# A new written-out order for an RWKV attention with Fourier mixing, and a last output tile in two halves

## The chip, the cores and the metric

The kernel runs on one core of one Trainium2 chip. The time is that of the device for one execution, in microseconds (us), as the median of several runs. A profile is taken of one execution by the hardware profiler, and its time is given beside its span, the time from the first to the last instruction. The engines are TensorE (PE, matmuls), VectorE (DVE), ScalarE (ACT), GpSimd (POOL) and SyncE (SP, which here only issues DMAs).

## The reference

Inputs are r, k and v of 4 batches, 8 heads, 768 tokens and 48 channels, a decay w and a bonus u per head and channel, and the weights of an MLP. The first part is a linear attention with a decaying state, the second a Fourier mixing over tokens and channels, a normalisation and an MLP with a residual:

```python
for t in range(S):
    cur = np.einsum('bhd,bhe->bhde', u[None] * kt, vt)
    y[:, :, t] = np.einsum('bhd,bhde->bhe', rt, state + cur)
    state = w[None, :, :, None] * state + np.einsum('bhd,bhe->bhde', kt, vt)
...
x = np.ascontiguousarray(attn_out.transpose(0, 2, 1, 3)).reshape(B, S, H * D)
X = np.fft.fft(np.fft.fft(x, axis=1), axis=2)
u = x + np.real(X).astype(np.float32)
un = (u - mu) / np.sqrt(var + 1e-06)
ch = np.maximum(un @ w_ch1, 0.0) @ w_ch2
return (u + ch).astype(np.float32)
```

The output has 4 x 768 rows of 384 columns in f32; the hidden layer of the MLP has 1536 columns.

## The kernel before

**Attention.** Each batch is cut into 6 chunks of 128 tokens, so there are chunks 0 to 23, six for each batch. For a chunk SP loads k, r and v (192 KB each; a ring of four buffers for k with r, and one of four for v). In the first twelve chunks DVE multiplies k and r by powers of the decay in two steps, KK (line 337) and KR (line 341); from chunk 12 on in one step, KR (line 330). Up to chunk 14 PE turns both round (tp, line 357) into one PSUM buffer, and two copies bring them to SBUF: KT, the keys (line 372), and KRT, the row copy of r, which also changes the order of the tokens by a strided access (line 375). From chunk 15 on SP's DMA transposes do this. V is a cast of v to bf16 (line 349 on ACT, 350 on DVE). PE forms the scores A (line 392) in two PSUM buffers; each half is masked into MA, on DVE straight from PSUM (line 404), or on POOL (line 401) after a copy AC by ACT (line 399). PR (line 382) is a product that gives the bonus term; de (lines 456 and 461), y (line 481), TT (lines 469 and 472), DE and xt put the chunk's result together in PSUM, and X (line 490 on DVE, 493 on ACT) brings it out in bf16. The state S is updated by u (line 424) and copied by DVE (line 438) or ACT (line 436).

**Mixing.** DVE folds X over tokens and channels by sums and differences: HH (line 510) and XF (line 524) for batch 0; EO (line 544), HH (line 550) and XF (lines 558 and 563) for the others. The matmuls fp (line 601) with the table te transform over tokens, TT2 copies the result out (line 610 on ACT, 613 on DVE), TR is that result reversed (line 620 on DVE, 624 on ACT), and mp (line 641) with the table hid transforms over channels. A batch gives two halves of three tiles. UF (lines 654 and 660) adds the residual X; where ACT does it, a matmul xr (line 652) adds X in PSUM first. UB is the normalised bf16 copy, and st and MV the statistics, either bn_stats and bn_aggr on DVE or a square with a sum on ACT (line 674). UNT is UB turned round, by PE (tq, line 685) in batch 0 and by SP's DMA transposes in the others.

**MLP.** Each of the 8 halves (numbers 0 to 7, two for a batch) has 12 times hp (three matmuls with W1, line 733) and HT, the ReLU (line 738 on ACT, 741 on DVE), and three output tiles: mo (12 matmuls with W2, line 753), osb on DVE (line 760) and the output DMA from SP (line 764). The two weight matrices come in by three POOL DMAs each (line 791), and each of these waits for the data of a certain chunk by a small copy before it (line 790). Most PSUM tiles of the mixing and the MLP share a ring of three buffers named mm.

**The order.** Nothing is scheduled while the kernel is built. Every operation is recorded with `op(...)`: a name, an engine, a planned duration, and other forms on other engines. It is then emitted in the order of a text:

```python
def _order(sch):
    return [(int(t.split(".")[0]), int(t.split(".")[1]) if "." in t else 0) for t in ORDER.split()]
...
        for n, a in order:
            o = self.ops[n]
            ...
            o["alts"][a][3]()
```

A token such as 226.1 stands for operation 226 in its other form, so the text sets both the order on every engine's queue and which engine does the work. Each engine takes its instructions in the order of emission. Operations 0 to 89 are filler matmuls on zeros (`idle`, line 211); those whose number is in the text are run.

Of the kernel before, what the change touches and what calls it, by code (L numbers as in the profile page):

```python
# [15 lines left out]
B = 4  # L16
# [3 lines left out]
DM = 384  # L20
# [73 lines left out]
106 93 144 90 94 113 101 120 95 110 118 146 97 137 102 91 92 115 98 0 105 103 114 104 1 143 96 140 116 147 117 2 107 99 108 112 111 3 149 109 4 5 150  # L94
119 6 121 7 130 152 124 8 122 128 9 125 148 10 221 129 11 222 100 145 126 132 224 123 241 151 133 242 12 13 225 14 153 226.1 15 131 142 227 228 155
139 134 127 244 265 231.1 235 223 232.1 16 156 236.1 17 245 233 246.1 18 229 158 234 19 20 135 237.1 248 230 136 154 138 141 239.1 251.1 266 238 21
157 243.1 268 249 247 253 252.1 22 159 269 250 23 270.1 24 254.1 25 289 272 161 240.1 290 26 273.1 275 255 274.1 162 292 267 256.1 276 257.1 27 160
293 277 271 259.1 291 258 278 28 163 260.1 309 301 294 310 279 164 302.1 296 333 312 280 218 297.1 298.1 299 281 29 30 313 314.1 31 165 334 283 282
311 316 315 321 167 295 317.1 336 335 261 32 284 300 337 33 34 338.1 319 303 285 35 168 262 322.1 304.1 36 305.1 37 981 38 219 318.1 307.1 306 220 263
340 170 264 39 355 341.1 166 308.1 725 286 726 343 342.1 320 323 739 718 324.1 325.1 344 732 740 719 327.1 339 326 356 733 328.1 288 287 345 329 171  # L100
734 330 720 346.1 741 347.1 727 169 332 349.1 331 348 375 721 350.1 173 742 722 395 743 735 736 174 352 728 351 729 357 353 354 376 172 723 744 737
724.1 980 367 745 730 176 738.1 731 358 396 368.1 177 748 746 754 377 747 749 755.1 179 750 760 982 756.1 387 761 762 774 388.1 775.1 359.1 780 776.1
751.1 786 781 757.1 360 787 763.1 768 415 777 378 782 180 769.1 983 362 379 788 175 794 365 783.1 772 789 770 795 361 796 773.1 771 366 369 363 797
798 370 986 799 380 364 752.1 1010 381 178 398 416 764.1 753.1 181 1008 399.1 371 987 765.1 382 1009 1040 397.1 400 373 383.1 384.1 407 385 372 418
435 1011 402 436 419 1002 1041.1 405.1 403 386 1026 408 420 182 404 1012 374 1027 438 1003 406.1 183 389 439 417.1 422 401 184 390 1000 421 437 425.1
423.1 426.1 1013 391 427 185 988 465 440.1 1006 428.1 441 186 424.1 393.1 984 392 989 447 1001.1 394.1 442 188 448.1 463 1034 464 443 189 409 1035.1
466 410 758.1 411 1007.1 1038 445 467.1 759.1 998 413 487 1039 412 766.1 1022 999 414 468 996 488.1 1023 429 469 497 997 191 470 767 444 498 430 778.1
1036 471.1 431 473.1 474.1 192 992 784.1 779.1 489 505 790.1 187 785.1 433.1 994 490 791.1 1037.1 446 432 190 995.1 1014 985 434.1 472.1 993 507 194
792.1 449 1015 491 492 508.1 195 450 1004 451 495.1 493 496.1 1028 197 1005 509 1024 1029 523 453.1 452 1025 1016 454.1 793 494 990 1017 475 455 991
1078 541 476 506 515 198 456 510 524 1079 477 511.1 512.1 513 543 516.1 457 525 458 479.1 478 526 193 1018 459 196 461 460 480.1 1019 558 199 583 533  # L110
499 528 500 1066 200 482 529 481 1080 531 501 201 1067 542 1020 484 560 545 462 559 1068 532 503.1 502 800 801 504.1 483 808 202 804 584 485 805 517
1081 486 809 534 530 802 518 806 810 803 550 514 807.1 811 203 812 604 813 546 814 1042 815 204 816 548 544 818 206 551 519 817.1 1043 819 820 1069
527 567 821 824 1044 549 521.1 568.1 585 520 825 826 547 830 522.1 839 831 561 605 851 840 832 207 562 827 852 552 1021 841 565.1 833 845 613 853
843.1 1030 846 847 838 553 842 844.1 1031 854.1 822.1 848.1 586 859 828.1 823.1 566.1 1054 554 834.1 829.1 556 555 563 205 1032 1055 835.1 849.1 1045
557 836.1 621 587 850.1 855.1 535 1046 590 1056 856.1 209 1074 536 614 1047 537 1076 857.1 208 1075.1 588 1070 858 539 1077.1 210 1082 1071 837 638
1098 1083 606 1106 1099 1084 1107 538 212 1085.1 1060 622 564 213 540 1048 589 1061 1062 1049 639.1 569 591 1063 630 640 1096 631.1 655 1110 1097 1108
607 1033 1111 1058 570 1109 211 571 1094 1059 1112 1095 573 672 1100 623 1113 572 608 1101 574 1052 611.1 609 612.1 214 1086 1053 217 575 592 1087
1072 576 656 1050 641 1073 1057 577 642 593 1051 578 1064 645.1 643 674 646.1 594 647 1088 1065 648 1114 596 1089 579 215 582 216 580 595 581 1102 673
597 610 599 1115 598 601 600 1103 603 602 1116 644 615 1126 657 616 1104 697 1127 1117 675 1105 860 861 617 1128 862 864 865 863 866 625 624 619 1129
867 618 628.1 872 698.1 626 873 620 874 868 869 875 876 870 1150 629.1 627 871 877 878 658 1151 879 880 881.1 882.1 649 1152 884 699 650 659 883.1 651  # L120
885 886 890 662.1 660 899 891 892 1153 653 664 887 661 900 905 901 893 911 906 907 652 902 912 1138 898 913 903.1 908.1 1090 914 904.1 665 909.1 663.1
919 1139 894.1 654 910.1 915.1 700 895.1 676 1140 683 916.1 917.1 679.1 677.1 1091 678.1 1141 684 888.1 685 680.1 1118 889.1 896.1 1092 687 686 1134
1119 918 688 1093 1122 1135.1 632 1123.1 1154 633 897 634 701 1155.1 1120 702.1 704 636 681 635 1121 1142 705 637 682.1 1130 703.1 1143 666 1146
1131.1 667 668 1148 1147 1178 1149 670 669 1132 1179 671 1124 1133 689 706 1125 690 1144 707 1136 691 1145 1170 692 1137 1162 708 1171.1 693 1168 710
696 709 695 1163 1169 694 711 1174 713 712 1164 1175 714 1165 715 717 920 716 921 928 1176 922 929 930 923 932 1177 933 931.1 934 924 925 935 926 1158
927 1172 1159 936 938 937 1173 944 939 940 945.1 950 946.1 1182 951 952 941 1160 947.1 1183 953.1 959 1161 965 958 960 961 942.1 971 966 967 1186 962
972 943.1 973 968 1187 954.1 974.1 979 963.1 955.1 1156 1188 975.1 964.1 1180 1157.1 1189 948.1 1184 976.1 1181.1 1166 1185 949.1 1190 969.1 1167.1
1204 1191.1 956.1 970.1 977.1 1208 1205.1 1196 957 1209 978 1216 1197 1226 1217 1214 1227 1220 1215.1 1228 1221 1194 1229.1 1206 1195 1202 1207 1192
1203 1232 1193 1198 1233.1 1199 1218 1200 1234 1219 1201 1235 1256 1236 1210 1257 1237 1211 1240 1212 1246 1241.1 1213 1247 1252 1248 1250 1253.1 1249
1238 1251 1230 1239 1258 1231 1259 1242 1260 1244 1243 1261 1270 1245 1254 1266 1255.1 1271 1267 1272 1273 1262 1268 1269 1222 1223 1263 1224 1225  # L130
1264 1265
"""


# [5 lines left out]
def kernel(  # L140
# [177 lines left out]
    def attend(i):  # L318
# [45 lines left out]
        else:  # L364
# [5 lines left out]
            else:  # L370
                def keys(copy):
                    return lambda: copy(KRT()[:, 0], tp()[:, 0])
# [467 lines left out]
```

## Time and profile before

| What | Value |
|---|---|
| Median of 5 runs | 181.57 us (180.8 to 183.18) |
| Profiled execution | 180.8 us, span 178.8 us, mean granted TensorE clock 0.996 |
| PE busy | 163.9 us (92%), of this 13.1 us filler matmuls (40 instructions) |
| DVE busy | 140.7 us (79%) |
| ACT busy | 118.8 us (66%) |
| POOL busy | 43.9 us (25%) |
| DMA | 26.84 MB moved, mean 150 GB/s |

Busy times are sums over the whole span; the share of an engine in one stage can be quite different, so the prediction reads them by stage. Times within the run are counted from the start of the span. Matmul records are pipelined, and one lasts longer than the time from its start to the next start.

### The profile page before, as it was taken

How to read it: one execution, taken by the hardware profiler on the slowest of the kernel's cores; microseconds unless marked ns; L12 is line 12 of the kernel's file. 1: busy time of each engine (PE TensorE's matmuls, PEld its weight loads, DVE VectorE, ACT ScalarE, POOL GpSimd, SP SyncE). 2: the span in 40 equal slices, each digit the busy share in tenths (PEclk: the TensorE clock that was granted, in tenths of full speed). 3: DMA queues.
4: the chain of work that ended last, by engine and by line, in shares of the span. 5: the costliest groups of instructions: out<-in, count | busy, mean ns of one | idle time of the engine just before them, and what ended most of it. 6: DMA issues, size and time to landing. Idle time of an engine off the chain costs nothing.

```text
span 178.8 us, 4317 instructions
## 1 busy us (share of the span) xinstructions
PE 163.9 (92%) x1628; PEld 108.4 (61%) x1628; DVE 140.7 (79%) x338; ACT 118.8 (66%) x290; POOL 43.9 (25%) x66
## 2 busy tenths in 40 slices
PE   5877968898999999999999899999999999999991
PEld 2344646675766666677666567766667765656560
DVE  5699899998999999999975999998696972232222
ACT  2897973399999994689989634595834997313200
POOL 6011335025344640742151133304210000000000
PEclk9999999999999999999999999999999999999998
DMA  3999899999999998999999998283002170022122
GB/s 81 240 219 223 193 277 213 212 229 226 198 183 178 181 185 160 181 207 244 150 241 215 141 208 215 45 189 101 0 0 91 29 149 0 18 73 88 44 88 88
DMA packets 88900, 26.84 MB, mean 150 GB/s; under 512 B 80432, under 2 KB 88240, under 8 KB 88880
## 3 DMA queue, kind: packets, MB, share of 16 engines
q1 hardware_dynamic: 86176, 23.77, 61.9%
q0 software_dynamic: 2144, 2.36, 8.2%
q10 hardware_dynamic: 560, 0.44, 0.8%
q8 instruction: 12, 0.20, 0.5%
q14 instruction: 8, 0.07, 0.1%
HBM read 20.08 MB, written 4.72 MB: 139 GB/s over the span
## 4 chain that ended last, share of the span: by engine, by line
PE 56%; DVE 15%; DMA 11%; ACT 8%; issue 3%; SPq 2%; POOL 2%; ACTq 0%; DVEq 0%; POOLq 0%
PE mm L753 23%; PE mm L733 19%; DMA W<-in_moe_w_ch_dram 4%; DMA vt<-in_v_dram 4%; PE mm L641 4%; PE mm L601 3%; DMA lw<-in_w_dram 3%; DVE MA L404 2%; SPq L306 2%; PE A_ps L392 2%; DVE KRT L375 2%; DVE PR L382 2%; DVE HH L550 1%; PE yd_ps L481 1%; DVE KR L341 1%
## 5 line engine op out<-in xcount | busy, mean ns | idle before, releaser
L733 PE MATMUL mm<-UNT,W 128*128 128x384 bf16 x288 | 53.4, 326 | 0.8 <-ACT DE L467 0.6
L753 PE MATMUL mm<-W,HT 128*128 128x384 bf16 x288 | 51.0, 326 | 0.4 <-DMA W<-in_moe_w_ch_dram 0.4
L738 ACT ACTIVATE HT<-mm 128x384 bf16<-128x384 f32 x71 | 34.1, 495 | 15.8 <-PE mm L733 15.7
L753 PEld LDWEIGHTS <-HT 128*128 128x128 bf16 x288 | 27.3, 98 | 17.4 <-issue 0.7
L733 PEld LDWEIGHTS <-W 128*128 128x128 bf16 x288 | 26.6, 97 | 17.1 <-issue 1.1
L469 POOL TENSOR_TENSOR TT<-V,DE 128x384 bf16<-128x384 bf16 x19 | 16.8, 884 | 48.9 <-ACT DE L467 48.2
L760 DVE SCALAR_TENSOR_TENSOR osb<-mm,rstd,UF 128x384 f32<-128x384 f32 x24 | 14.6, 614 | 14.9 <-PE mm L753 14.9
L401 POOL TENSOR_SCALAR_AFFINE_SELECT MA<-AC 128x512 bf16<-128x512 bf16 x26 | 18.7, 729 | 28.6 <-ACT AC L399 22.2
L741 DVE TENSOR_SCALAR HT<-mm 128x384 bf16<-128x384 f32 x25 | 13.3, 551 | 7.3 <-PE mm L733 7.2
L399 ACT CAST AC<-A_ps 128x512 bf16<-128x512 f32 x26 | 15.3, 593 | 2.6 <-PE A_ps L392 2.3
L674 ACT ACTIVATE lw<-UF,sm 128x384 f32<-128x384 f32 x24 | 14.8, 616 | 1.7 <-DVE UF L654 1.4
L404 DVE TENSOR_TENSOR MA<-A_ps,mtri 128x512 bf16<-128x512 f32 x22 | 14.9, 681 | 0.0
L211 PE MATMUL mm<-zero 128*128 128x512 bf16 x40 | 13.1, 449 | 1.9 <-DVE zero L227 1.9
L330 DVE TENSOR_TENSOR KR<-kr,tab 128x768 bf16<-128x768 f32 x12 | 12.6, 1058 | 2.4 <-DMA kr<-in_r_dram 2.4
L601 PE MATMUL mm<-te_t,XF 128*128 128x193 bf16 x99 | 11.9, 247 | 1.1 <-DVE XF L524 0.5
L392 PE MATMUL A_ps<-KRT 64*128 64x128 bf16 x192 | 9.9, 218 | 2.8 <-DVE KRT L375 2.5
L654 DVE SCALAR_TENSOR_TENSOR UF<-mm,X 128x384 f32<-128x384 f32 x21 | 11.0, 553 | 0.7 <-PE mm L641 0.5
L601 PEld LDWEIGHTS <-XF 128*128 128x128 bf16 x120 | 9.8, 97 | 2.6 <-DVE XF L524 1.1
L382 DVE TENSOR_TENSOR PR<-KRT 128x512 bf16<-128x512 bf16 x24 | 10.8, 455 | 0.4 <-ACT KRT L375 0.3
L610 ACT CAST TT<-mm 97x386 bf16<-97x386 f32 x11 | 6.2, 602 | 7.1 <-PE mm L601 7.1
L481 PEld LDWEIGHTS <-MA 128*128 128x128 bf16 x192 | 8.1, 96 | 4.5 <-issue 1.2
L357 PE MATMUL tp<-ident,KR 128*128 128x128 bf16 x120 | 9.5, 219 | 1.1 <-DVE KR L337 0.7
(97 smaller groups left out, 247.6 us busy)
## 6 DMA issues: line engine op xcount, KB each, us to landing
kr<-in_k_dram SPq DMA_DIRECT2D x24, 192.0 KB, 4.7
vt<-in_v_dram SPq DMA_DIRECT2D x24, 192.0 KB, 4.1
out_dram<-osb SPq DMA_DIRECT2D x24, 192.0 KB, 2.1
kr<-in_r_dram SPq DMA_DIRECT2D x23, 192.0 KB, 4.8
W<-in_moe_w_ch_dram POOLq DMA_DIRECT2D x6, 384.0 KB, 6.3
te_t<-te_c SPq DMA_DIRECT2D x1, 579.0 KB, 5.6
hid_t<-hid_c SPq DMA_DIRECT2D x1, 288.0 KB, 6.9
lw<-in_w_dram ACTq DMA_DIRECT2D x1, 192.0 KB, 3.8
```

The costliest lines, as they stand in the source:

```text
L382: op(("PR", i), "DVE", 410, lambda: nc.vector.tensor_tensor(out=PR(), in0=KRT()[:, 0], in1=KRT()[:, 1], op=AluOp.mult), r=[("KRT", i)] + k ...
L392: nc.tensor.matmul(A_ps[a]()[:, p, :], lhsT=KRT()[rows, 0, p, :], rhs=KRT()[rows, 1, p, :], start=(p == 0), stop=(p == NP - 1), skip_group ...
L399: op(("AC", i, a), "ACT", 590, lambda: nc.scalar.copy(AC(), A_ps[a]()), r=[("A", i)], w=[("AC", i, a)], new=[AC], use=[A_ps[a]], pri=pri, ...
L401: op(("MA", i, a), "POOL", 630, lambda: nc.gpsimd.affine_select(out=MA[a](), in_=AC(), pattern=[[0, NP], [1, 128]], base=0, channel_multip ...
L404: port=True, other=[("DVE", 680, False, lambda: nc.vector.tensor_tensor(out=MA[a](), in0=A_ps[a](), in1=mtri.unsqueeze(1).to_broadcast([12 ...
L469: op(("TT", i), "POOL", 830, lambda: nc.gpsimd.tensor_tensor(out=TT(), in0=V(), in1=DE().unsqueeze(2).to_broadcast([128, H, D]), op=AluOp. ...
L601: nc.tensor.matmul(fp()[:, par, :], lhsT=lhsT[:, g * CH:g * CH + 128], rhs=rhs, start=(nb == 0 and par == 0), stop=(nb == last and par == ...
L674: other=[("ACT", 720, False, lambda: nc.scalar.activation(out=lw, in_=UF()[:, j, :], func=Act.Square, scale=-float(DM), bias=sm()[:, j:j + 1],
L733: nc.tensor.matmul(hp(), lhsT=W1[:, dt, ft * 128:(ft + 1) * 128], rhs=UNT()[:, :, dt, :], start=(dt == 0), stop=(dt == 2))
L738: op(("HT", hf, ft), "ACT", 495, lambda: nc.scalar.activation(out=HT()[:, ft, :], in_=hp(), func=Act.Relu, scale=-1.0), r=[("hp", hf, ft)] ...
L753: nc.tensor.matmul(mo(), lhsT=HT()[:, ft, j * 128:(j + 1) * 128], rhs=W2[:, ft, :], start=(ft == 0), stop=(ft == 11))
L760: op(("osb", hf, j), "DVE", 620, lambda: nc.vector.scalar_tensor_tensor(out=osb(), in0=mo(), scalar=rstd()[:, j:j + 1], in1=UF()[:, j, :], ...
```

## The change

ORDER is replaced by another text. It holds 39 filler matmuls instead of 40 and all other operations, with another order and for more than a hundred of them the other form. In the first batch these operations change engine: the row copies KRT of chunks 0, 1, 2, 4 and 5 go from DVE to ACT, the key copies KT of chunks 0 and 3 from ACT to DVE, the casts V of chunks 0 and 2 from ACT to DVE, the product TT of chunk 2 from POOL to DVE, the reversals TR from DVE to ACT, and three masks each way between DVE and ACT with POOL. On SP the loads are ordered anew: te and hid stand before k of chunk 6 instead of after it and after r of chunk 7, v of chunk 0 stands before r of chunk 1, and v of chunks 6 to 8 before r of chunk 8.

Four planned durations change, which `emit` does not read, and the last output tile (half 7, tile 2) is computed in two parts, columns 0 to 191 and 192 to 383, each with its own PSUM tile, matmuls, osb and output DMA. In the new text the second part's matmuls come some tiles before the end and the first part's last of all.

```diff
 ORDER = """
-106 93 144 90 94 113 101 120 95 110 118 146 97 137 102 91 92 115 98 0 105 103 114 104 1 143 96 140 116 147 117 2 107 99 108 112 111 3 149 109 4 5 150
...
+94 93 144 90 115 113 120 95 101 146 116 97 102 91 92 110 114 104 96 0 107 105 103 1 143 106 99 118 147 2 112 137 108 111 117 98 3 140 149 109 4 5 148
...
+1196 1241 1254 1197 1262 1255 1246 1247 1266 1248 1249 1263 1267 1264 1265 1274 1268 1275 1269 1234 1276 1277 1258 1259 1235 1260 1261 1270 1236 1271
+1237 1272 1273
 """
...
-            op(("KR", i), "DVE", 560, lambda: nc.vector.tensor_tensor(
+            op(("KR", i), "DVE", 600, lambda: nc.vector.tensor_tensor(
...
-                op(("KT", i), "ACT", 570, keys(nc.scalar.copy), r=[("tp", i)], w=[("KT", i)], new=[KRT], use=[tp], pri=pri,
+                op(("KT", i), "ACT", 590, keys(nc.scalar.copy), r=[("tp", i)], w=[("KT", i)], new=[KRT], use=[tp], pri=pri,
                    other=[("DVE", 430, False, keys(nc.vector.tensor_copy))])
-                op(("KRT", i), "ACT", 570, row(nc.scalar.copy), r=[("tp", i)], w=[("KRT", i)], use=[KRT, tp], pri=pri,
-                   after=[("KT", i)], other=[("DVE", 430, False, row(nc.vector.tensor_copy))])
+                op(("KRT", i), "ACT", 620, row(nc.scalar.copy), r=[("tp", i)], w=[("KRT", i)], use=[KRT, tp], pri=pri,
+                   after=[("KT", i)], other=[("DVE", 690, False, row(nc.vector.tensor_copy))])
...
+        parts = [slice(0, DM)] if (hf, j) != (2 * B - 1, 2) else [slice(0, 192), slice(192, DM)]
+        for c, cols in enumerate(parts):
+            tag = (hf, j) if len(parts) == 1 else (hf, j, "c", c)
+            n = cols.stop - cols.start
+            mo = new(ps, [128, n], F32, "mm", 3)
+            osb = new(wp, [128, n], F32, "osb", 3)
...
+                    nc.tensor.matmul(mo(), lhsT=HT()[:, ft, j * 128:(j + 1) * 128], rhs=W2[:, ft, cols],
+                                     start=(ft == 0), stop=(ft == 11))
...
+                out=osb(), in0=mo(), scalar=rstd()[:, j:j + 1], in1=UF()[:, j, cols], op0=AluOp.mult, op1=AluOp.add),
...
+            op(("out", *tag), "SP", 420, lambda osb=osb, cols=cols: nc.sync.dma_start(out=out[b, row:row + 128, cols], in_=osb()),
```

## The prediction

> **What bounds the kernel now.** I read the page first (shares, slices), then the busy times by stage, then the groups of the first batch, the waits, and the timeline of the end. The stages are mine: tables up to 9 us, the first batch's attention up to 36, its transform to 45, a mixture up to 68, then the long part in which TensorE (PE) has matmuls of both kinds to choose from, and from 138 the last MLP.
>
> ```profile
> PE 163.9 (92%) x1628; PEld 108.4 (61%) x1628; DVE 140.7 (79%) x338; ACT 118.8 (66%) x290; POOL 43.9 (25%) x66
> ...
> PE   5877968898999999999999899999999999999991
> ...
> DVE  5699899998999999999975999998696972232222
> ...
> DMA  3999899999999998999999998283002170022122
> ```
>
> ```profile
> core 0: us, PE busy (x) PEld busy (x) DVE busy (x) ACT busy (x) POOL busy (x), PEclk, DMA share, GB/s
> ...
> 9.00:36.00 27.00, 21.60 (x289) 15.14 (x288) 25.93 (x64) 18.43 (x40) 7.09 (x13) 1.00 1.01 223
> 36.00:45.00 9.00, 8.04 (x100) 6.07 (x97) 8.19 (x26) 8.64 (x25) 3.34 (x5) 1.00 1.14 227
> 45.00:68.00 23.00, 21.85 (x275) 14.91 (x270) 22.96 (x46) 21.91 (x58) 10.75 (x14) 1.00 1.01 182
> 68.00:100.00 32.00, 31.64 (x339) 21.62 (x337) 27.89 (x61) 26.78 (x65) 10.58 (x13) 1.00 1.06 201
> 100.00:138.00 38.00, 37.24 (x381) 25.38 (x380) 34.08 (x81) 21.40 (x55) 9.31 (x12) 1.00 0.45 109
> 138.00:175.30 37.30, 37.23 (x240) 22.87 (x238) 15.77 (x38) 16.61 (x41) 0.00 (x0) 1.00 0.22 59
> ```
>
> In the second fence the first number is the length of the stage, then each engine's busy time. PE runs at the full granted clock throughout. Whole stages after 36 us leave it idle for 0.96 + 1.15 + 0.36 + 0.76 + 0.07 = 3.3 us in all. In 9 to 36 it is idle 5.4 us, and 7.4 us more of its busy time there are the 26 filler matmuls of line 211, which compute nothing (the same windows for that line alone): 12.8 us of 27 without work. So there is room in the first batch, and nearly nowhere else. In that stage VectorE (DVE) is busy 25.93 of 27 us and ScalarE (ACT) 18.43: DVE sets the pace. The DMA share is about 1 up to 110 us, so data comes at the DMA's own rate.
>
> **The change, part by part.** The new planner costs (600, 590, 620, 690 for 560, 570, 570, 430) are not read when the order is emitted: ORDER is a text. They cost nothing. No line of the diff touches a table. What counts is who does what in the new ORDER, and the last tile.
>
> *First batch, up to the first transform of the residual.* DVE loses five row copies (KRT of chunks 0, 1, 2, 4, 5, line 375) and the two reversals TR (line 620), which go to ACT; it gains the key copies KT of chunks 0 and 3 (line 372), the casts V of 0 and 2 (350) and the product TT of chunk 2 (472, from GpSimd). Three masks, one state and one X go each way and cancel.
>
> ```profile
> L375 DVE COPY KRT<-tp 128x512 bf16<-128x512 bf16 x6 | 4.1, 685 | 0.8 <-ACT KRT L372 0.8
> ...
> L375 ACT COPY KRT<-tp 128x512 bf16<-128x512 bf16 x6 | 3.7, 612 | 0.0
> ...
> L472 DVE TENSOR_TENSOR TT<-V,yd_ps 128x384 bf16<-128x384 bf16 x5 | 2.7, 544 | 0.0
> L620 DVE COPY TR<-TT 97x768 bf16<-97x768 bf16 x7 | 2.5, 385 | 1.1 <-ACT TT L610 1.1
> ...
> L350 DVE CAST V<-vt 128x384 bf16<-128x384 f32 x6 | 2.1, 349 | 0.0
> ...
> L372 DVE COPY KRT<-tp 128x512 bf16<-128x512 bf16 x3 | 1.2, 417 | 0.0
> ...
> L624 ACT COPY TR<-TT 97x768 bf16<-97x768 bf16 x1 | 0.9, 872 | 0.0
> ```
>
> These are groups by form; after the bar stand busy us, mean ns of one, and idle before. The row copy is strided and takes DVE 685 ns against 417 for the key copy; ACT needs 612 and 592 for them. DVE: out 5 x 0.685 + 2 x 0.385 = 4.20, in 2 x 0.417 + 2 x 0.349 + 0.544 = 2.08, net -2.1 us. Neighbours on DVE overlap by some 0.085 us (KR at 16.80 and 17.27 take 0.55 each), and two instructions fewer are left: -1.9 us. ACT gets 5 x 0.612 + 2 x 0.872 less 2 x 0.592 + 2 x 0.518 and a DE, about +2.4 us; its 8.6 idle us in this stage hide that. Without that cover it would cost 2.4. Also, KR of 6 and KK of 7 and 8 (1.4 us of DVE) now stand behind the transform's folds instead of ahead, so the queue in front of the last fold shrinks by 2.6 us, but these three come due in the next stage.
>
> The Trainium skill speaks against one move: "ScalarE: Activation LUTs", section "Rules for kernel authors", has simple elementwise work done on VectorE, up to about three times faster per element in bf16. The reversal's rows, 385 ns against 872, agree in kind; by the rule alone both reversals would be a loss of 1 us, by the rows only where ACT has no idle time.
>
> *36 to 64 us.* By the fold EO of batch 1 (64.4 us before) the DVE gets back a part: three statistics of half 0 move from ACT squares (0.616 + 0.193 each) to bn_stats and bn_aggr on DVE, which no row shows. Nearest passes over the same 384 columns: 0.476 (line 667) and 0.614 (line 760), for the small one 0.16 (line 710); I take 0.55 + 0.16, nearer to the passes that read f32 in SBUF or PSUM at 0.55, so 3 x 0.71 = 2.1 (1.9 to 2.3). All other swaps there (HT, KT, V, UNT, masks) give -0.8. Net +1.3, with overlap +1.0; ACT -1.4. So up to 64 us DVE's work is smaller by 0.9 us only, while it is busy 22.96 of 23. Two ends for the gain at 68 us: 0.9, if DVE limits all of it, and 2.6, if only the queue before the transform counts. I take 1.9: PE, not DVE, ends last in that stretch as long as matmuls are there, it lost only 1.15 us in 45 to 68, and MLP matmuls now start earlier in its queue (two hp ahead of the last tq).
>
> *Queues.* On SP, te (landed 1.8 us after its predecessor) and hid (1.0 us) now go ahead of the loads k 6 to r 7, v 0 goes ahead of r 1, and v 6 to 8 ahead of r 8. By the trace's DMA records k 6 landed at 22.5 and was used at 27.9; 2.8 us later is 25.3, in time even if DVE asks at 26. On POOL, W1's second and third load no longer stand behind the mask of chunk 5, so 1.6 MB of reads move from 29 to about 25 us into the same full stream. Cover is about 1 us; value 0, bounds 0 to +2.
>
> *After 68 us.* The gain can't exceed the 1.2 us that PE still loses there; a loss is bounded by the rival below. Value 0. Filler matmuls: 39 for 40, in idle time. The matmul xr (line 652, 0.17 us from start to start) is added twice in batch 3 and dropped once: +0.17; one more in batch 0 falls where PE is idle anyway. Three more statistics move to DVE at 143 to 146 us, where DVE is busy 15.77 of 37.3: hidden.
>
> *The last tile in two halves.* Four matmuls of 192 columns (line 641) take 0.33 us from start to start, so 24 take 1.98 against 12 x 0.1625 = 1.95: +0.03. The skill's "TensorE: Matmul & The Clock Gate", section "Back-to-back issue gap", warns that the spacing is set by weight loads as well; with the row's 97 ns for a weight load it would be 2.33, +0.4, and line 641 with its own weight each shows that it isn't. Only the second half's evacuation and output stand behind the last matmul:
>
> ```profile
> 175.27 0.62 DVE L760 SCALAR_TENSOR_TENSOR osb<-mm,rstd,UF 128x384 f32<-128x384 f32 x1 [0.36 <-PE mm L753]
> ```
>
> An f32 product of 384 columns takes 0.55 and of 768 1.06, so 192 fewer columns save 0.25 of 0.62 us. An output takes 1.8 us at least and 2.1 in the median from issue to landing; no row has half of one. Bounds 0 and 0.42 (half of the 0.85 us between landings of 192 KB in the full stream); I take 0.2, since an almost idle queue shows mostly latency. Tail: -0.42.
>
> Sum: -1.9 + 0.17 - 0.42 = **-2.15 us**. The profiled execution had 178.8 us of span and 2.0 around it, 180.8; the median of the five is 181.57 and 0.8 above. Against the median: 179.4 us.
>
> **The rivals.**
>
> ```profile
> DVE KR L330 <- DMA kr<-in_r_dram: 2.4, 2, 1.9
> ...
> ACT V L349 <- DMA vt<-in_v_dram: 2.1, 4, 1.4
> ```
>
> *A: given back.* DVE is full from 45 to 68, and later loads set the pace: r 21 landed at 93.85 and was used at 93.88, r 23 at 108.50 and 108.60; the waits (us in all, times, longest) are these. Then only 0.9 of the 1.9 remains: 180.4. If data is late in the first batch as well (2 us at k 6), 181.4. Against it: DVE idles 4.1 of 32 us after 68, and SP's stream is held up by its own transposes, which would move up too.
>
> *B: slower, at the first transform of batch 1.* In the old order PE has 6.7 us of work between y of chunk 11 (68.7 us) and the fp matmuls that need its fold (76.0 us), and still waits 0.67. In the new one there are 2.1 us: one half mo, de, four fp, A. The chain X, EO, HH, XF is 0.48 on ACT and six DVE instructions, about 2.4 us, if DVE is free. If its queue is as full as now (X at 69.6, last XF done at 75.9: 6.3 us), PE waits 4.2: 179.4 + 4.2 = 183.6. It decides from a DVE lag of some 2 us. Against it: in the new queue nothing else stands between these six.
>
> *C: the order does on the chip nothing that its planner saw.* Only the tail counts: 181.3.
>
> **How the numbers follow.** Forecast 0.55 (own range 178.0 to 180.4; 0.48 of it below 179.75, one per cent under the median), A and C together 0.31, B 0.14 (0.01 of it within one per cent). The range leaves out the outer ends: 177.4 (2.6 for 1.9, 0.7 for 0.42, and 1.0 of the later waits gone) to 183.0 (B in part). One per cent, 1.8 us, is about what a measurement of this kernel can tell from no change. Faster 0.48, same 0.39, slower 0.13.
>
> **What would show it.** Right: DVE's row copies gone before 36 us, the first hp matmul before 41 us (42.7 now), PE without work 9 to 36 down from 12.8 to about 11, last osb near 0.36 us. Wrong: a DVE wait for k 6; a PE wait over 1 us at the fp of batch 1; more than 3 us of idle PE after 68.

## The result and the profile after

The kernel after takes 182.02 us in the median of 38 executions, the kernel before 181.46 us in 75; the ratio is 0.9998, 95% interval 0.9975 to 1.0022. The change makes no difference that can be measured. Executions of either kernel spread over 4 to 5 us (179.4 to 184.7 after, 179.9 to 184.2 before); ratios leave out those more than 1.5% above the fastest of their kernel, medians do not. Both profiles of after are of executions above that spread, 185.12 us with a span of 183.3 here and 185.14 in run 1 below, while that of before is of 180.8 us. So they show the losses larger than the median execution can have them, and the main readings are set beside run 6, which has the same order up to 77 us in an execution of 181.3 us.

First the page of after (busy tenths in 40 slices of the span), then its busy times by stage, and line 211, the filler matmuls, in 9 to 36 us alone.

```profile
PE 165.4 (90%) x1641; PEld 109.3 (60%) x1641; DVE 143.1 (78%) x348; ACT 117.8 (64%) x281; POOL 44.3 (24%) x67
...
PE   5798988789999899599699959999999999999993
...
PEclk9999999999999999999999978999999999999999
```

```profile
core 0: us, PE busy (x) PEld busy (x) DVE busy (x) ACT busy (x) POOL busy (x), PEclk, DMA share, GB/s
9.00:36.00 27.00, 23.55 (x311) 16.70 (x310) 25.41 (x67) 21.57 (x47) 6.61 (x12) 1.00 1.02 224
36.00:45.00 9.00, 7.86 (x94) 5.46 (x93) 8.97 (x27) 8.58 (x22) 3.12 (x5) 1.00 1.08 213
45.00:68.00 23.00, 21.82 (x272) 14.69 (x271) 20.32 (x40) 19.76 (x52) 11.74 (x15) 1.00 1.02 183
68.00:100.00 32.00, 27.90 (x297) 19.11 (x296) 27.80 (x62) 23.65 (x59) 10.10 (x14) 1.00 1.07 189
100.00:138.00 38.00, 35.88 (x357) 23.34 (x356) 32.45 (x71) 23.10 (x59) 9.91 (x12) 0.96 0.50 110
```

```profile
9.00:36.00 27.00, 6.99 (x24) 1.90 (x23) 1.00 1.02 224
```

In the first batch PE is without work for 27 - 23.55 + 6.99 = 10.4 us, where it was 12.8. So the step that was meant to gain does gain. From 68 to 138 us PE is idle for 4.1 + 2.1 = 6.2 us, where it was 1.1, and the granted clock in 100 to 138 is 0.96, where it was 1.00. What is gained ahead is lost there. The slices say where: fives and sixes at 73, 87 and 105 us in a row that had only nines and one eight there, and a seven and an eight in PEclk. The waits of PE name what it waits for (us in all, times, longest):

```profile
PE mm L601 <- DVE XF L563: 2.5, 1, 2.5
PE mm L758 <- DVE HT L741: 2.1, 2, 1.9
...
PE mm L733 <- DMA UNT<-UB: 1.1, 1, 1.1
...
PE A_ps L392 <- ACT KRT L375: 0.5, 1, 0.5
```

The first is the fp of batch 1, the second mo of half 3, the third the first hp of half 2; the last is the scores' wait for KRT. Before, the second and the third were not there, and the first and the last read:

```profile
PE A_ps L392 <- DVE KRT L375: 2.5, 3, 1.1
...
PE mm L601 <- DVE XF L563: 0.5, 2, 0.3
```

The scores waited for DVE, which is the queue that the move of the row copies shortened. The waits for loads have grown as well:

```profile
DVE KR L330 <- DMA kr<-in_r_dram: 4.6, 4, 1.8
ACT V L349 <- DMA vt<-in_v_dram: 4.5, 5, 1.4
...
DVE KR L337 <- DMA kr<-in_k_dram: 1.1, 1, 1.1
```

They were 2.4, 2.1 and none. The end of the timeline (start, us, engine, line):

```profile
179.29 0.62 DVE L765 SCALAR_TENSOR_TENSOR osb<-mm,rstd,UF 128x384 f32<-128x384 f32 x1 [0.36 <-PE mm L758]
180.28 0.42 DVE L765 SCALAR_TENSOR_TENSOR osb<-mm,rstd,UF 128x192 f32<-128x192 f32 x1 [0.37 <-PE mm L758]
```

The last evacuation takes 0.42 us instead of 0.62, and the span ends 183.3 - 180.70 = 2.6 us after it instead of 2.9.

For the rest one number is followed through the traces: how long PE has been without work up to a certain matmul. It is the start of that matmul less the work done before it, each group of matmuls counted at the spacing that it has in the trace of before, fillers at nothing.

| Profile | first mp of batch 0 | u of chunk 13 | last part of the first fp, batch 1 | first fp, batch 2 |
|---|---|---|---|---|
| about, us | 32 to 36 | 64 to 67 | 74 to 77 | 108 to 114 |
| before | 22.4 | 26.7 | 28.1 | 29.7 |
| after | 18.5 | 25.2 | 28.2 | 34.4 |
| after, run 1 | 18.7 | 25.8 | 29.7 | 33.5 |

The lead, the difference to before in a column, is 3.8 us at the first batch's transform and, in these two profiles, 1 to 1.5 us at 66 us and nothing at the fold of batch 1.

### The profile page after: what moved, and what is told of

Same layout as the page of the kernel before. It is cut to its first block, busy times and chain, and to the rows that moved or that the text cites. A ratio compares the mean times of both kernels' runs of the same rounds, so it can differ in the third digit from the quotient of the medians.

```text
span 183.3 us, 4346 instructions
## 1 busy us (share of the span) xinstructions
PE 165.4 (90%) x1641; PEld 109.3 (60%) x1641; DVE 143.1 (78%) x348; ACT 117.8 (64%) x281; POOL 44.3 (24%) x67
## 4 chain that ended last, share of the span: by engine, by line
PE 42%; DMA 21%; DVE 20%; ACT 9%; SPq 3%; issue 2%; ACTq 0%; DVEq 0%
PE mm L758 20%; PE mm L733 12%; DMA kr<-in_r_dram 10%; DMA kr<-in_k_dram 7%; PE mm L601 3%; DVE HH L550 3%; PE mm L641 3%; DMA UNT<-UB 2%; DMA lw<-in_w_dram 2%; DVE KR L330 2%; ACT HT L738 2%; ACT AC L399 2%; ACT UB L663 2%; DVE KR L341 2%; SPq L299 2%
## 5 line engine op out<-in xcount | busy, mean ns | idle before, releaser
L758 PE MATMUL mm<-W,HT 128*128 128x384 bf16 (+1 forms) x300 | 52.0, 326 | 2.1 <-DVE HT L741 2.1
L738 ACT ACTIVATE HT<-mm 128x384 bf16<-128x384 f32 x67 | 32.5, 495 | 16.2 <-PE mm L733 16.1
L758 PEld LDWEIGHTS <-HT 128*128 128x128 bf16 x300 | 28.5, 99 | 19.7 <-DVE HT L741 2.3
L733 PEld LDWEIGHTS <-W 128*128 128x128 bf16 x288 | 26.4, 97 | 16.9 <-issue 1.5
L401 POOL TENSOR_SCALAR_AFFINE_SELECT MA<-AC 128x512 bf16<-128x512 bf16 x28 | 20.1, 727 | 33.7 <-ACT AC L399 19.4
L765 DVE SCALAR_TENSOR_TENSOR osb<-mm,rstd,UF 128x384 f32<-128x384 f32 (+1 forms) x25 | 14.9, 599 | 15.7 <-PE mm L758 14.6
L469 POOL TENSOR_TENSOR TT<-V,DE 128x384 bf16<-128x384 bf16 x18 | 15.8, 880 | 41.6 <-ACT DE L467 29.6
L741 DVE TENSOR_SCALAR HT<-mm 128x384 bf16<-128x384 f32 x29 | 15.4, 552 | 5.0 <-PE mm L733 4.9
L404 DVE TENSOR_TENSOR MA<-A_ps,mtri 128x512 bf16<-128x512 f32 x20 | 13.4, 683 | 0.3 <-PE A_ps L392 0.2
L674 ACT ACTIVATE lw<-UF,sm 128x384 f32<-128x384 f32 x18 | 11.1, 618 | 0.2
L349 ACT CAST V<-vt 128x384 bf16<-128x384 f32 x15 | 7.5, 514 | 4.9 <-DMA vt<-in_v_dram 4.5
L654 DVE SCALAR_TENSOR_TENSOR UF<-mm,X 128x384 f32<-128x384 f32 x19 | 9.9, 555 | 0.9 <-PE mm L641 0.7
```

The source lines that it names most:

```text
L401: op(("MA", i, a), "POOL", 630, lambda: nc.gpsimd.affine_select(out=MA[a](), in_=AC(), pattern=[[0, NP], [1, 128]], base=0, channel_multip ...
L404: port=True, other=[("DVE", 680, False, lambda: nc.vector.tensor_tensor(out=MA[a](), in0=A_ps[a](), in1=mtri.unsqueeze(1).to_broadcast([12 ...
L469: op(("TT", i), "POOL", 830, lambda: nc.gpsimd.tensor_tensor(out=TT(), in0=V(), in1=DE().unsqueeze(2).to_broadcast([128, H, D]), op=AluOp. ...
L733: nc.tensor.matmul(hp(), lhsT=W1[:, dt, ft * 128:(ft + 1) * 128], rhs=UNT()[:, :, dt, :], start=(dt == 0), stop=(dt == 2))
L738: op(("HT", hf, ft), "ACT", 495, lambda: nc.scalar.activation(out=HT()[:, ft, :], in_=hp(), func=Act.Relu, scale=-1.0), r=[("hp", hf, ft)] ...
L741: other=[("DVE", 560, False, lambda: nc.vector.tensor_scalar(out=HT()[:, ft, :], in0=hp(), scalar1=-1.0, scalar2=0.0, op0=AluOp.mult, op1= ...
```

## The experiments

Four theories were put up in the course of it. L: the loads of later chunks land on their own clock, so what is ahead of them waits for them. Q, later called B: the new order's own queues give the lead back, above all at the fold of batch 1, where PE has little work left. G: the stretches at half clock cost the time. W: only the waits themselves do.

**Run 1: after once more**, to see whether its profile was a disturbed one.

> The changed kernel once more, for a second profile. Theory L (the loads keep their own clock): the first batch ends 2 to 4 us earlier than before, r of chunk 16 and 17 land within 1.5 us of the old 67.8 and 69.2 us, DVE waits for r somewhere in 50 to 70 us, and PE waits 2 us or more at the fp matmuls of batch 1 near 75 us; time within 0.5% of before. Theory Q (only the queue order, PE has too little work between y of chunk 11 and fp): the same PE wait, but DVE's KR of 16 and 17 start without waiting for data. Theory N (the wait of the first profile was a disturbed run): no PE wait over 1 us at that fp.

Measured: 182.15 us, ratio 0.9963 (0.9925 to 1.0002), and a wait of 2.47 us at the same matmul. The wait belongs to the kernel: it stands in runs 6, 10 and 17 below as well, in executions of 181.3, 181.5 and 178.6 us. The loads r 16 and r 17 landed at 67.7 and 69.6 us and were used 0.1 us later, as L had it and Q had not.

**Run 2: KR of chunks 16 and 17 behind the fold.** In after DVE waits for r 16 and r 17 (landed at 66.5 and 68.1 us) with the fold's instructions queued behind.

```diff
 EO 1.0.0  EO 1.0.1
-KR 16
 HH 1.0.0  HH 1.0.1
-KR 17
 ...
 XF 1.2.1  XF 1.2.0
+KR 16  KR 17
 S 15
```

> The changed order with two tokens moved: KR of chunks 16 and 17 stand behind the last XF of batch 1 in DVE's queue instead of ahead of its folds. Theory L: the fold no longer waits for r of 16 and 17, PE's wait at fp of batch 1 falls from 2.5 us to under 1 us, and the time goes down by 1 to 2 us (ratio to before 0.988 to 0.996), unless the matmuls of chunk 16 then wait instead. Theory Q: the fold chain is still longer than PE's 2.1 us of work; the PE wait stays above 1.5 us and the time stays at 0.997 to 1.003.

Measured: 183.96 us, 1.0105 (1.0051 to 1.0158). The wait at the fold is still there, and one of its size has come up behind it, because S 15 now stands behind the two KR (PE's waits). It was moved, not removed:

```profile
PE mm L601 <- DVE XF L563: 2.6, 2, 1.9
...
PE u_ps L424 <- DVE Sst L438: 1.9, 1, 1.9
```

**Runs 3 to 6: mixes of the two orders.** Up to a cut the new order, after it all that is left in the old order: at 320 tokens (about 37 us, whole last tile), 380 (43 us, last tile in halves), 540 (62 us, in halves) and 619 (77 us, whole).

```diff
-ORDER = old
+ORDER = new[:cut] + [t for t in old if t not in new[:cut]]
```

> The first batch and the start of its transform from the new order (its first 320 tokens), everything else in the old order, last tile whole. Theory L: the first transform begins 2 to 4 us earlier, the loads up to r of 17 do not, and PE's work runs out before the fp matmuls of batch 1: time 0.995 to 1.003 of before. Theory Q: with the old rest, where 6.7 us of PE work cover the fold of batch 1, the gain of the first batch stays: 0.985 to 0.992.

> The same with the change of order at 380 tokens (about 43 us): the new first batch alone with the transform's tail, then the old order. Theory B: as the cut at 540 or up to 1 us longer, 0.98 to 0.995. Theory L: 0.995 to 1.005, with the gain gone by 60 us.

> The new order up to 540 tokens (to about 62 us, ahead of the fold of batch 1), then the old order, in which more matmuls stand between y 11 and the fp of batch 1; last tile in two halves. By the profiles PE has lost 2 to 3 us less than in the old order by then. Theory B (the gain is given back by the new order's own fold): it is kept, no PE wait over 1 us at fp of batch 1, mean clock 0.995 or more, ratio 0.98 to 0.99. Theory L (from 45 us on loads and DVE set the pace, and old or new order makes no difference): PE waits elsewhere in 62 to 100 us, ratio 0.995 to 1.002.

> The new order up to the first transform of batch 1 (619 tokens, to about 77 us), then the old order for the rest, last tile whole. Theory P (what is lost after 77 us comes from the new order of the later part: waits at hp of half 2, mo of half 3, the fold of batch 2): those waits go, ratio about 0.993 to 0.999, idle PE from 100 to 138 us back under 1 us. Theory Q (all of it comes from the low PE use at the fold of batch 1): that wait of 1.9 to 2.5 us and the stretch at half clock behind it stay, 0.998 to 1.005.

| Cut | us | ratio (95%) | u of 13 | fp, batch 1 | fp, batch 2 |
|---|---|---|---|---|---|
| 320 | 183.07 | 1.0071 (1.0037 to 1.0106) | 28.8 | 30.4 | 31.5 |
| 380 | 180.74 | 0.9978 (0.9938 to 1.0019) | 26.1 | 27.8 | 29.6 |
| 540 | 182.09 | 0.9969 (0.9913 to 1.0026) | 24.5 | 29.8 | 31.8 |
| 619 | 182.34 | 1.0048 (1.0009 to 1.0087) | 23.4 | 27.2 | 29.9 |

(The right-hand columns are PE's time without work, as above; in 380 and 540 to about 0.2 us.) All four had a lead of nearly 4 us at the first mp. No mix keeps it beyond the fold of batch 1, the one with the old order's fold (540) no more than the others, so a bad fold in the new order isn't the whole cause: the ratios for 380 and 540 lie in L's ranges and above B's. The cut at 320 is above both ranges: it adds waits of PE in 36 to 40 us, where the old order's rest doesn't fit, and a stretch at half clock. At 619 the later waits of the new order are gone, as theory P said, but the time is no shorter than that of after, as Q said: the wait of 2.47 us at the fold and half clock behind it stay.

The cut at 619 also shows what the two profiles of after do not. With the same order up to 77 us its u of 13 starts at 64.6 us (64.6, 65.4 and 65.0 in runs 15, 10 and 9, which share the order up to there), where the two of after start it at 66.4 and 67.1. So 3.3 us of the lead, not 1 to 1.5, are left at 66 us, and it is lost from there to the fold: 0.9 is left. In between PE waits 0.67 us for X 11, which stands on ACT behind the casts V 14 and V 15 (their loads land at 67.7 and 69.7 us), and the 2.47 us for XF. DVE waits for r 2.8 us in all, in after 4.6, and is busier in 45 to 68 us:

```profile
45.00:68.00 23.00, 22.82 (x282) 15.60 (x282) 21.75 (x42) 20.39 (x53) 11.00 (x15) 1.00 1.06 191
```

With the cut at 540 ACT stood still for a load in the middle of the fold:

```profile
ACT V L349 <- DMA vt<-in_v_dram: 7.0, 2, 5.1
```

**Runs 7 and 8: wide rows.** k, v, and r from chunk 12 on are loaded in rows of 768 bytes instead of 192, in after and in before; other tokens come to each partition, so the output is another.

```diff
-nc.sync.dma_start(out=vt(), in_=v[b, :, sl, :].rearrange("h p d -> p h d"))
+nc.sync.dma_start(out=vt().rearrange("x (a j) d -> x a (j d)", a=2), in_=v[b, :, sl, :].rearrange("h (p j) d -> h p (j d)", j=4))
```

> The changed kernel with k and v of all chunks, and r of chunks 12 to 23, loaded in rows of 768 bytes as r of chunks 0 to 11 is: a quarter of the DMA packets, the same bytes, tokens in another order inside a chunk (the output is not the reference's). To be read beside the old kernel with the same loads, which runs next. Theory L: with loads that land earlier the gain of the first batch comes through, so this is faster than the old kernel with wide loads by 2 us or more, and the DMA share falls below 0.9 after 30 us. Theory Q: the two wide kernels differ by less than 1 us, as the two originals do.

> The kernel before with the loads of k, v and (from chunk 12 on) r in rows of 768 bytes, the counterpart of the same edit on the kernel after (186.85 us, 1.0165); other tokens come to each partition, so the output is another. Theory L: with the same loads the kernel after is at least 2 us faster than this one, so this takes 188.5 or more. Theory B: the two differ by under 1.5 us, as with narrow rows: 185.5 to 188.

Measured: after 186.85 us (1.0165, 1.0099 to 1.0232), before 186.42 us (1.0255, 1.0197 to 1.0313). The medians are alike and the ratios 0.9% apart with intervals that overlap. It settles nothing: in after the wide rows took the DMA share in 9 to 36 us from 1.0 to 0.85 but moved the same 225 GB/s, and the first transposes began later (8.7 us against 6.9), so the loads were not out of the way.

**Runs 9 and 10: the fold mended.** TT, xt, y of chunk 11 go ahead of mo 1.1, X 11 ahead of the cast V 14, KR 17 behind S 15; in run 10 also HT 5 of half 3 ahead of the XF of batch 2.

```diff
 mo 1.2.1
+TT 11  xt 11  y 11
 mo 1.1.1
 ...
+X 11
 V 14
 ...
 S 15
+KR 17
```

> The kernel after with the fold of batch 1 mended: TT, xt, y of chunk 11 ahead of mo of half 1 tile 1 (they stood behind u 14, which waits for the load of v 14), X 11 on ACT ahead of the cast V 14, KR 17 on DVE behind S 15. Theory B (the gain of the first batch is given back at this fold, because X 11 comes late and PE has only 2.2 us of work between y 11 and the fp that need the fold): the wait of 2.5 us at fp of batch 1 falls under 1 us, fp there at 73 to 74.5 us, mean clock up by about half a per cent, ratio to the kernel before 0.985 to 0.995. Theory L (loads land on their own clock): the same matmuls wait later for r 18 to r 21 or v, the time stays, 0.996 to 1.003.

> The same, and on DVE HT 5 of half 3 ahead of the XF of batch 2 (PE waited 1.0 to 1.9 us for it at 106 us, mo of half 3). Theory B: 1 to 1.9 us less than the kernel with the fold alone, 0.978 to 0.99. Theory L: the wait moves to the fold of batch 2 (fp at 112 us), within 0.5 us of the kernel with the fold alone.

Measured: 183.64 us, 1.0136 (1.0081 to 1.019), and 183.57 us, 1.0103 (1.0046 to 1.016). Run 9 falls outside every range; run 10 lies 0.1 us from it by the medians, as L had it, though PE's wait for HT 5, 1.9 us in after, is gone from its trace. In run 9 the wait at the fold fell to 1.07 us, but u of chunk 14 now waits for its V, whose load lands at 70.7 us; in run 10 it is 2.47 again, with y 11 done 3 us ahead of where it was. Why the two are slower than after by more than 1 us stays open. So when y 11 is done doesn't set it. The timelines show what differs, DVE and then GpSimd (POOL), first after:

```profile
71.82 0.62 DVE L544 TENSOR_TENSOR EO<-X 128x384 bf16<-128x384 bf16 x2
72.48 1.57 DVE L550 TENSOR_TENSOR HH<-EO 128x384 bf16<-128x384 bf16 x2
74.15 1.32 DVE L563 TENSOR_TENSOR XF<-HH 128x392 bf16<-128x392 bf16 x2
...
72.13 1.00 POOL L469 TENSOR_TENSOR TT<-V,DE 128x384 bf16<-128x384 bf16 x1 [5.26 <-ACT DE L467]
73.09 2.17 POOL L401 TENSOR_SCALAR_AFFINE_SELECT MA<-AC 128x512 bf16<-128x512 bf16 x3
```

and run 9:

```profile
72.43 0.63 DVE L550 TENSOR_TENSOR HH<-EO 128x384 bf16<-128x384 bf16 x2
73.40 1.30 DVE L563 TENSOR_TENSOR XF<-HH 128x392 bf16<-128x392 bf16 x2 [0.34 <-PE mm L601]
...
72.94 0.83 POOL L469 TENSOR_TENSOR TT<-V,DE 128x384 bf16<-128x384 bf16 x1 [6.91 <-ACT DE L467]
```

The two HH take 0.63 us when they start with GpSimd still, and 1.57 us when the first starts inside its product TT 12 and the second inside the mask behind it. The two XF take 1.32 us here, inside the next two masks, and 0.76 us at 112.99 us of after, with GpSimd still. Each of the four ends 0.21 to 0.22 us after the GpSimd instruction inside which it starts: the first HH at 73.35 for 73.13 us, the last XF at 75.47 for 75.25. It is so in runs 1, 6, 10 and 17 too, and in all of them the wait is 2.47 us. That is 1.5 us of it, and it speaks for TT 12 and its three masks, not DVE's queue, as what the fold waits for; this is read from traces, and no run took them away.

**Run 11: the mended fold with the cut at 619**, last tile in halves.

> The new order up to 77 us with the fold mended in the same way, then the old order for the rest, last tile in two halves. Theory B: the first batch's gain (2.4 us) is kept, the later waits of the new order are not there, tail -0.5: ratio 0.98 to 0.99, the shortest of these three. Theory L: 0.995 to 1.0, with PE waits for DVE behind late loads in 77 to 110 us in place of the one at the fold.

Measured: 181.56 us, 0.9988 (0.9949 to 1.0027). L's range holds, B's does not. In its profile (an execution of 184.3 us) the wait at the fold is 2.47 us again, so the fold was not mended there.

**Run 12: the last tile alone**, in the old order.

```diff
-mo 7.0.0 ... mo 7.0.1 osb 7.0 out 7.0                      (the last tile of the old order)
+mo 7.2.c1 osb 7.2.c1 out 7.2.c1 mo 7.2.c0 ... osb 7.2.c0 out 7.2.c0
```

> The old order with the last tile alone changed: the tile in two halves of columns is the last of all, its second half just ahead of the first. Both theories: the tail term alone, -0.42 us, ratio 0.9977 (0.995 to 1.000); in the profile the last osb takes 0.42 instead of 0.62 us and the span ends about 2.6 us after it instead of 2.9. Mean clock 1.00 as before. If the whole change's gain in the first batch is lost again, this part alone is not slower than the whole.

Measured: 181.21 us, 0.9970 (0.993 to 1.001). The forecast of 0.9977 lies well inside, though so does no change. The last osb takes 0.41 us as forecast, but the span ends 2.85 us after it, not 2.6. The two halves' outputs follow each other at once here, as in the cuts at 380 and 540 and in run 11, with 2.84 or 2.85 in each; in after, where the second part goes out some tiles earlier, it is 2.63.

**Runs 13 to 15: the granted clock.** In run 13, 27 matmuls on zeros stand inside four waits of after; in run 14 19 fillers are taken out of before; in run 15, 12 zeros stand in the wait at the fold of run 6, and nothing else is changed.

```diff
+                if (b, g, nb) == (1, 0, 2):
+                    for _ in range(12):
+                        nc.tensor.matmul(fp().rearrange("p a n -> p (a n)"), lhsT=zero[:, 0:128], rhs=zero[:, 0:386],
+                                         start=False, stop=False, skip_group_check=True)
                 for par in range(2):
```

> The kernel after, with matmuls on zeros added inside four waits of TensorE (14 ahead of the last part of the first fp of batch 1, 5 ahead of the mp of tile 3 of batch 0, 2 ahead of the first hp of half 2, 6 in mo of half 3 ahead of the sixth piece of HT; 0.16 us each, together 4.3 us; they add zero or are overwritten). Theory G (the granted clock): the profile of after has stretches of 3.5 us at half clock soon after a stretch in which PE was busy less than about half of the time (108 to 111.5 us; in the second profile 76 to 79.7), and its executions show a mean clock of 0.99 or 0.98, where the kernel before shows 1.00. With the waits filled the mean clock goes back to 0.995 or more and the time falls by about 1.7 us per stretch: ratio to the kernel before 0.985 to 0.993. Theory W (only the waits themselves count): the filled waits end when they did, nothing is gained and up to 1 us of zeros is lost where the data comes early: 0.998 to 1.006, whatever the clock.

> The kernel before without 19 of its 40 filler matmuls (those at 12.5 to 26 us). Theory G: the fillers keep the busy share of every 3.4 us above about 0.65; without them it falls to about a half in 12 to 26 us, one to three stretches at half clock follow, mean clock 0.97 to 0.99, and the time rises by 0.5 to 3 us: ratio 1.003 to 1.017. Theory W: fillers only take up idle time of PE, where DVE sets the pace; the time stays or falls by up to 0.5 us: 0.996 to 1.001.

> The splice at 619 tokens (new order to 77 us, old order after it, whole last tile; 182.34 us, 1.0048, mean clock of its executions 0.984) with 12 matmuls on zeros, 0.16 us each, in the wait of 2.5 us at fp of batch 1; nothing else is changed. Theory G (the stretch at half clock behind this wait costs time): mean clock to 0.99 or more, 0.9 to 1.7 us less: 0.995 to 1.0. Theory W (only the wait counts): clock up, time the same within 0.5 us, 1.002 to 1.008.

Run 13: 184.89 us, 1.0132 (1.0059 to 1.0205), though its profile has a clock of 1.00: both theories miss. The zeros are 4.3 us of work, and its waits are partly elsewhere (1.2 us at a u for a V that came late). Why it loses as much as 2.4 us against before isn't settled. Run 14: 182.38 us, 1.0060 (1.0026 to 1.0095), mean clock over its executions 0.970 instead of 0.997, with two stretches at half clock in its trace (17.8 and 28.0 us): as G said, though 0.027 of 180 us is 4.9 us of clock and the time rose by 1.0; in those stages DVE was seen to set the pace. Run 15 is the clean one: against run 6 the mean clock goes from 0.984 to 0.996 and the ratio from 1.0048 to 1.0004 (0.9967 to 1.004), 0.6 us in the medians. That is just above G's range and below W's, and the two intervals overlap, so it isn't clear of noise. Half clock behind the fold is then a part of it at most, of the order of half a microsecond.

**Runs 16 to 18: light loads.** From chunk 6 on k, r and v bring two of the eight heads (the rest is what chunks 2 to 5 left in four fixed buffers, so the output is another): before, after, and the cut at 380.

```diff
+    def HL(i):
+        return 8 if i < 6 else 2
-nc.sync.dma_start(out=vt(), in_=v[b, :, sl, :].rearrange("h p d -> p h d"))
+nc.sync.dma_start(out=vt()[:, 0:HL(i)], in_=v[b, 0:HL(i), sl, :].rearrange("h p d -> p h d"))
```

> The kernel before with lighter loads: from chunk 6 on k, r and v bring two of the eight heads (48 KB instead of 192 KB each); the others keep what chunks 2 to 5 left in the four fixed buffers, so the output is another; the order and all other work are the same. 7.8 of 26.8 MB less. Both theories: waits for loads go; at most the 3 us that PE loses after 36 us, and some of the first batch: ratio 0.97 to 1.0.

> The kernel after with the same lighter loads. Theory L (the gain of the first batch is lost because the loads of the later chunks land when they did): with the loads out of the way it is kept, 2 us or more under the kernel before with lighter loads (1.1 per cent of ratio or more between the two). Theory B (the new order's own queues give it back, whatever the loads): within 1 us of it, and the wait of about 2.5 us at fp of batch 1 stays.

> The cut at 380 tokens (new first batch, old order from about 43 us, last tile in two halves) with the same lighter loads. Theory L: 2 to 4 us under the kernel before with lighter loads. If VectorE sets the pace from 45 us on and not the loads: within 1 us of it, apart from the tail's 0.5.

| Light loads | us | ratio (95%) | first mp | u of 13 | fp, batch 1 | fp, batch 2 |
|---|---|---|---|---|---|---|
| before | 179.93 | 0.9914 (0.9881 to 0.9946) | 22.3 | 26.3 | 28.0 | 28.7 |
| after | 178.75 | 0.9838 (0.9791 to 0.9886) | 18.3 | 22.0 | 25.0 | 27.1 |
| cut at 380 | 178.47 | 0.9843 (0.9795 to 0.9892) | 18.6 | 24.7 | 26.3 | 27.0 |

Now the lead of after is still 4.3 us at u of 13, where with full loads 3.3 was left in run 6 and 1 to 1.5 in the two profiles of after. At the fold it is 3.0, where 0.9 was left in run 6. The stages of it, and the wait at its fold:

```profile
36.00:45.00 9.00, 8.46 (x103) 5.77 (x101) 8.91 (x25) 8.93 (x25) 3.95 (x7) 1.00 0.53 79
45.00:68.00 23.00, 22.83 (x285) 15.73 (x284) 22.44 (x44) 20.05 (x51) 10.37 (x14) 1.00 0.53 82
68.00:100.00 32.00, 29.33 (x306) 20.52 (x304) 28.76 (x63) 24.83 (x63) 11.00 (x15) 0.95 0.76 131
```

```profile
PE mm L606 <- DVE XF L568: 3.2, 2, 2.5
```

From 36 to 68 us PE is idle for 0.7 us, in run 6 1.3 and in after 2.3, with half the DMA share. The loads' part is then some 2 us by the fold: the lead falls there from 4.0 to 3.0 us instead of from 3.8 to 0.9. The wait of 2.5 us at the fold stays and a stretch at half clock follows it (0.95 in 68 to 100); that is not the loads' part. After is 1.2 us shorter than before in the medians, some 0.5 of it the tail, neither the 2 us of L nor the 1 us of B, though the intervals of the two ratios overlap by a little. The cut at 380, which has the old fold, is 1.5 us shorter, and there they overlap. So both theories are right for a part.

## Why the prediction was wrong

*The bound, and the first batch: right, and undersized.* Room was in the first batch, and the step got it: the first mp starts at 31.7 us instead of 36.2, the first hp at 38.0 (under 41 was asked), five row copies and both reversals are off DVE. PE without work fell to 10.4 us in 9 to 36, about the 11 forecast; up to the first mp the lead is 3.8 us, more than the 1.9 to 2.6; the waits for KRT (2.5 to 0.5 us) and for TT fell too. ACT took 3.1 us more in that stage, which now holds some later work too, for the 2.4 forecast, inside its idle time, and a reversal there takes 842 ns: the rule that simple elementwise work belongs on VectorE, cited in the prediction, had no price here.

*36 to 64 us: the size held in run 6, the limit was another.* The sum took 1.9 us as kept at 68 us, because DVE, busy 22.96 of 23, seemed the limit, with the two ends 0.9 and 2.6. In after DVE is busy for 20.32 of these 23 us and in run 6 for 21.75: it isn't full, it waits, in after 4.6 us in all for r and, on ACT, 4.5 us for v. The statistics cost what was taken (550 + 173 ns), so the work was sized rightly; the loads were not in the sum. At 66 us 1 to 1.5 us of the lead is left in the two profiles of after, but 3.3 in run 6, more than the sum needs. So this term alone doesn't explain a time without gain. Rival A had the loads with the right view (r 21 used 0.03 us after it landed) and took 1 us for them; light against full loads gives them about 1 us up to 66 us and some 2 up to the fold, in run 6.

*Queues: right in place, wrong in size.* k 6 landed at 26.1 us and was used at 26.4, without a wait; k 7 was waited for, 1.1 us. What was missed is the cover of the loads behind them. In the trace of before r 8 to r 14 are used 3.2 to 7.6 us after they land, in that of after 0.1 to 1.4 us, r 11 apart; r 13 landed at 54.6 and was used at 58.4, and now lands at 57.6 and is used at 57.7. In run 6 it lands at 54.0 and the cover is 0.8 to 2.0 us. So the loads come little earlier for being wanted earlier (r 16 at 65.3 to 67.7 us instead of 67.8), with a DMA share of 1.0 in all of them.

*After 68 us: the step that failed.* The sum put this term at 0 and left a loss to rival B, at a chance of 0.14. In run 6 the lead falls from 3.3 to 0.9 us between 66 us and the fold of batch 1, 2.4 us; in the two profiles of after nothing is left there, and PE is idle for 6.2 us in 68 to 138 instead of 1.1 in the first of them. B's mechanism is what the trace shows: PE had 2.2 us of work (2.1 was forecast) between y 11 and the fp that need the fold. Its price was set for a full DVE queue, 4.2 us; measured is 2.47, from a chain of 4.7 us (X 11 to fp). The six DVE instructions of it, put at 2.4 us if DVE is free, take 3.65 with nothing else between them, since HH and XF end with GpSimd's instructions, 1.5 us later than alone, which no step foresaw. That the granted clock would drop behind such a wait wasn't in any step either, nor the wait of 1.9 us for HT 5 of half 3.

*The tail: right for this order.* -0.2 for osb and -0.3 for the output, -0.5 together for -0.42; with the tail alone in the old order (run 12) it is -0.2 and -0.1.

So the forecast failed where it put the time after 68 us at 0, and where it let A and B exclude each other: each was true in part, and by the fold of batch 1 they had together taken most of the lead or all of it. How much of what the profiles of after lose behind 77 us the median execution loses too stays open. Two of the three signs named for a wrong forecast are in the profile: a PE wait over 1 us at the fp of batch 1, and more than 3 us of idle PE after 68. The time, 182.0, lies between the outer ends of 177.4 and 183.0 but outside the forecast's own 178.0 to 180.4.

No order run here beats both kernels by more than can be told: the shortest, the cut at 380 with the tail (0.9978) and the tail alone (0.997), have intervals that reach 1.

## What to carry to other kernels

Before a loss is read from one profile, set it beside another execution of the same order: here the same matmul started between 64.6 and 67.1 us. A lead on the engine that ends last is worth nothing until the next thing that it meets is ahead too: compare, for each later load, when it landed with when it was used, since that gap and not the busy share is the cover that a gain upstream eats up. Count the work that the bounding engine has between the producer and the consumer of each long chain, and time the chain with its neighbours running, not free. To tell whether data or queues take a gain, make the data light in both kernels and compare the lead at the same instruction.

## What the hardware showed that had not been expected

**The granted clock can fall after waits of 2 us.** In after, PE waited 1.92 us from 105.9 us, and 2 us on this (windows of 1 us; the column before the last two is the granted clock):

```profile
107.00:108.00 1.00, 0.20 (x2) 0.14 (x3) 1.00 (x4) 0.00 (x0) 0.00 (x0) 1.00 1.08 260
108.00:109.00 1.00, 1.00 (x5) 0.53 (x4) 0.97 (x4) 0.00 (x0) 0.00 (x0) 0.55 1.13 305
109.00:110.00 1.00, 1.00 (x9) 0.55 (x7) 1.00 (x3) 0.00 (x0) 0.00 (x0) 0.50 0.04 14
110.00:111.00 1.00, 1.00 (x6) 0.47 (x4) 1.00 (x3) 0.17 (x1) 0.61 (x1) 0.50 0.00 0
111.00:112.00 1.00, 1.00 (x7) 0.49 (x5) 0.58 (x2) 0.00 (x0) 0.22 (x1) 0.75 0.39 80
```

Such a stretch lasts about 3.5 us. The wait of 2.47 us at 73 us in the same execution was followed by none; in runs 1, 6, 10, 11 and 17 it was. So it comes in some executions and not in others: over the executions of one series the mean clock was 0.997 for before and 0.988 for after. The Trainium skill's "TensorE: Matmul & The Clock Gate", section "HAM oscillation — how this bites in real kernels", warns of idle gaps over about 3.4 us; here the wait before the stretch was 1.92 us.

**DVE products end with GpSimd's instructions.** The same two HH take 0.63 or 1.57 us, by the lines above, as GpSimd stands still or works when they start, and then end 0.2 us after its instruction. The skill's "Trainium Architecture — The Big Picture", section "What this means for kernel authors", has the two engines share a port by an exclusive lock, which agrees; no run here moved GpSimd's product and masks away to test it.
